# First weight conversions of a fused attention, soft-MoE and MLP kernel moved from GpSimd to VectorE and ScalarE

## Chip, cores and metric

The kernel runs on one core of a Trainium2 chip. The metric is the device time of one execution in microseconds. TensorE does the matmuls, VectorE, ScalarE and GpSimd the elementwise work (in rows of the profile: PE, DVE, ACT and POOL; PEld is TensorE's weight load), and SyncE (SP) issues all the DMAs. Each engine works through its own instructions in order, and waits on semaphores for the others.

## What is computed

The reference chains three stages in float32, cut here to what matters:

```python
k_p, v_p = k.mean over 8 keys, v.mean over 8 keys
attn = softmax(q @ k_p.T / 8) @ v_p
x = attn as (4608 tokens, 512)

logits = x @ phi                       # 32 slots, 4 for each of 8 experts
d = softmax over tokens(logits)
slot_input = d.T @ x
slot_out[e] = relu(slot_input[e] @ w1[e]) @ w2[e]
c = softmax over slots(logits)
x = c @ slot_out

r = relu(x @ w_in)                     # 512 x 2048
out = (s * r * r + b) @ w_out          # 2048 x 512
```

In the last stage x = c @ slot_out has only 32 inner terms. So the kernel does not form x there: it multiplies slot_out into w_in first, S = slot_out @ w_in, and then h = c @ S.

## The kernel before

The attention and the routing come first and are not touched. Then comes the loop over the experts' weights, then the join, then the main loop.

**Experts.** EORD lists 32 weight tiles of 1 MB, and the loop of line 930 takes one in each step (step 0 to step 31). A w1 tile gives products into l1, a w2 tile gives one group of four matmuls into so_ps (line 947). Steps 22 to 31 are w2 tiles. The function hidden turns l1 into the experts' hidden values in three pieces; its last piece is the relu of line 923, and for the second half of the experts it stands at step 23. At the end of every step, step_convs moves each running generator by one piece and starts the next one from the queue todo. That queue holds the generators of combine_t: they take two or fewer tiles of combine weights each, cast them to float32r (cs, line 892), take the remainder on VectorE (line 893), and two steps later transpose both on TensorE (ct, line 898) and copy them to cT (line 904). A transpose is issued between two groups of expert products, so the groups behind it wait when its cs is late.

**Conversions.** The weights w_in and w_out lie in HBM as pairs of 32-bit words. The generator narrow makes float32 numbers of them. VectorE builds the high part in five operations (lines 818 to 828) in th and xp, ScalarE scales the low part into fr (line 830), GpSimd multiplies fr by xp (line 831) and adds it to th (line 832). conv_wi does this for a block of 128 columns of w_in, conv_wo for 128 rows of w_out; conv_wo also splits the result into whi (ScalarE, line 872) and wlo (GpSimd, line 874) and adds it to the column sums wsum (GpSimd, line 876 or 878). The main loop's first group needs two blocks of each (GROUPS[0] is 2). They are put at the front of todo at fixed steps: the two of w_in at steps 23 and 24 (WIPOS), the two of w_out at steps 26 and 27 (WOPOS), these only up to th.

**Join.** After the experts TensorE does two filler matmuls, ScalarE copies so_ps, TensorE sums it up (sot_ps), and then the string OPS orders what follows: `o` moves a w_out generator on by one piece, `a` and `b` are the two matmul steps of s_a and s_b that make a column block S, `h` is st_h (h = cT.T @ S, then relu and square into r), `g` is st_g, which splits r into gh (float32r) and the remainder gl. For step 0 of the main loop all this is done in halves of 384 tokens, the first half's relu and square on ScalarE and the second's on VectorE, and gh and gl of both halves on VectorE.

**Main loop.** Its 96 steps go over five groups of 2, 3, 3, 4 and 4 column blocks, six token blocks of 768 in each. In a step st_o does 18 matmuls of 512 columns (six token tiles, each gh with whi, gl with whi and gh with wlo, line 1073), and st_h and st_r prepare the step after the next. The later conversions are spread over the loop.

SyncE's queue holds the loads in the order of the list loads; a load waits until its buffer is free. Names that readers meet below: ring and raw are buffers of 1 MB (ring tiles that the experts are done with also hold th, xp and fr of the first four conversions), x a further set of such buffers.

The functions that the diff touches:

Of the kernel before, what the change touches and what calls it, by code (L numbers as in the profile page):

```python
# [13 lines left out]
ACTF = mybir.ActivationFunctionType  # L14
ALU = mybir.AluOpType
# [2 lines left out]

OPS = "o0 a0 o0 a1 b0 b1 h0 g0 o1 h1 o1 g1"
WIPOS, WOPOS = 22, 25  # L20
TAIL = "F0 6 C4 X0 D2 6 X1 E2 6 m 6 6 F2 D3 m D4 6 E4 6 m F4 X2 7 W3 7 W2 7 7 7 M2 6 7 7 M3 6 7 M4 7"
BUSY = (2, 0)
CUT = 1
# [33 lines left out]
def kernel(  # L57
# [14 lines left out]
    nc = tc.nc  # L72
# [9 lines left out]
    GROUPS = (2, 3, 3, 4, 4)  # L82
# [10 lines left out]
    raw = [cpool.tile([128, 2048], F32, name=f"raw{i}") for i in range(NRAW)]  # L93
# [12 lines left out]
    where = {}  # L106
# [656 lines left out]
    siz = None  # L763
    for op in TAIL.split():
        if op[0] in "FECD":
# [42 lines left out]
        scr_n[z] += 1  # L808
        return kept[k_][:, o_:o_ + 512].rearrange("p (a x) -> p a x", a=shp[1])

    def narrow(raw, dst):


        v = raw.rearrange("p a (x t) -> p a x t", t=2)
        lo, hi = v[:, :, :, 0], v[:, :, :, 1]
        shp = list(lo.shape)
        th, xp, fr = (scratch_of(z, shp) for z in ("th", "xp", "fr"))
        nc.vector.tensor_scalar(out=xp.bitcast(U32), in0=hi, scalar1=0x7FFFFFFF, scalar2=None, op0=ALU.bitwise_and)
        nc.vector.tensor_scalar(out=xp, in0=xp, scalar1=2.0 ** -15, scalar2=W_MAX, op0=ALU.max, op1=ALU.min)
        nc.vector.tensor_scalar(  # L820
            out=xp.bitcast(U32), in0=xp.bitcast(U32), scalar1=0x07FFFFFF, scalar2=3,
            op0=ALU.bitwise_and, op1=ALU.logical_shift_left,
        )
        nc.vector.scalar_tensor_tensor(
            out=th.bitcast(U32), in0=hi, scalar=0xC0000000, in1=xp.bitcast(U32),
            op0=ALU.bitwise_and, op1=ALU.bitwise_or,
        )
        nc.vector.tensor_scalar(out=xp.bitcast(U32), in0=th.bitcast(U32), scalar1=0xFF800000, scalar2=None, op0=ALU.bitwise_and)
        yield
        nc.scalar.activation(out=fr, in_=lo, func=ACTF.Copy, scale=2.0 ** -52)  # L830
        nc.gpsimd.tensor_tensor(out=fr, in0=fr, in1=xp, op=ALU.mult)  # L831
        nc.gpsimd.tensor_tensor(out=th if dst is None else dst, in0=th, in1=fr, op=ALU.add)  # L832
        yield th

    def conv_wi(f):

        gen = narrow(where["wi", f // 2][2][:, :, 256 * (f % 2):256 * (f % 2) + 256], None)
        next(gen)
        yield
        t = next(gen)  # L840
        if f % 2 == 1:
            done(("wi", f // 2))
        yield
        t_wi[f] = t
# [15 lines left out]

    def conv_wo(f):

        gen = narrow(where["wo", f // 2][2][:, f % 2:f % 2 + 1, :], None)
        next(gen)
        yield
        t = next(gen)[:, 0, :]
        if f % 2 == 1:
            done(("wo", f // 2))
        yield
        g, i = GOF[f]  # L870
        wh, wl = w_hi[g % 2][:, i, :], w_lo[g % 2][:, i, :]
        nc.scalar.copy(out=wh, in_=t)
        yield
        nc.gpsimd.tensor_tensor(out=wl, in0=t, in1=wh.bitcast(F32), op=ALU.subtract)
        if f == 0:
            nc.gpsimd.tensor_copy(out=wsum, in_=t)
        else:
            nc.gpsimd.tensor_tensor(out=wsum, in0=wsum, in1=t, op=ALU.add)

    convs, todo = [], deque()  # L880
# [28 lines left out]
    wo_ = [conv_wo(f) for f in range(GROUPS[0])]  # L909
# [20 lines left out]
    for n_, key in enumerate(EORD):  # L930
        w_, e, hf = key
        g, ge = divmod(e, EG)
        w = where[key][2]
        if w_ == "w1":
            for n in range(2):
                for c in range(2):
                    kc = 2 * hf + c
                    cg = (kc + 2 * n) % 4
                    nc.tensor.matmul(  # L939
                        out=l1[g][n][32 * cg:32 * cg + 32, :],  # L940
                        lhsT=siz[:, 128 * e + 32 * kc:128 * e + 32 * kc + 32],
                        rhs=w[:, c, 512 * n:512 * n + 512],
                        start=(ge == 0), stop=(ge == EG - 1),
                    )
        else:
            for c in range(4):
                nc.tensor.matmul(  # L947
                    out=so_ps[32 * c:32 * c + 32, :],
                    lhsT=h1z[:, 4 * hf + c, 36 * ge + 16 - 4 * e:36 * ge + 48 - 4 * e],
                    rhs=w[:, c, :],  # L950
                    start=(e == 0 and hf == 0), stop=(e == E - 1 and hf == 1),
                )
        done(key, 3 if n_ > 9 else int(n_ > 2))
        if n_ == BRIEF:
            brctx.close()
            cT_t.append(ctx.enter_context(tc.tile_pool(name="cv1", bufs=1, side="right")).tile([128, NTH], F32R, name="cT1"))
        if h1z is None and kept:
            h1z = kept[0][:, 0:1152].rearrange("p (f r) -> p f r", f=8)
            nc.gpsimd.memset(h1z, 0.0)
        advance(hid)  # L960
        if key == W1[g][-1]:
            hid.append(hidden(g))
            advance(hid)
        if WIPOS < n_ <= WIPOS + GROUPS[0]:
            todo.appendleft(conv_wi(n_ - WIPOS - 1))
        if WOPOS < n_ <= WOPOS + GROUPS[0]:
            todo.appendleft(islice(wo_[n_ - WOPOS - 1], 2))
        if key != EORD[-1]:
            step_convs()
    assert not todo, len(todo)  # L970
# [64 lines left out]
    def st_g(i, r):  # L1035
        if i == 0:
            gh = fp2.tile([128, 2, 384], F32R, tag="gh", name="gh")
        else:
            gh = gh_t.pop(i)
        gl = fp2.tile([128, 2, 384], F32R, tag="gl", name="gl")  # L1040
        for x in (slice(0, 1), slice(1, 2)) if i == 0 else (slice(0, 2),):
            if i == 0:
                nc.vector.tensor_copy(out=gh[:, x], in_=r[:, x])  # L1043
            nc.vector.tensor_tensor(out=gl[:, x], in0=r[:, x], in1=gh[:, x].bitcast(F32), op=ALU.subtract)  # L1044
        g_t[i] = (gh, gl)

# [50 lines left out]
    for op in OPS.split():  # L1097
        n = int(op[1])
        if op == "h1":
            r_[1] = st_h(1)  # L1100
            st_r(1, r_[1])
        elif op[0] == "a":
            s_a(n, scratch(2 * n))
        elif op[0] == "b":
            s_b(n, scratch(2 * n + 1))
        elif op[0] == "h":
            r_[n] = st_h(n)
        elif op[0] == "g":
            st_g(n, r_.pop(n))
        elif op[0] == "w":  # L1110
            busy(ps_o.tile([128, 512], F32, tag="o3", name="o3"), n)
        else:
            next(wo_[n], None)
    rctx.close()
    part_p = ctx.enter_context(tc.tile_pool(name="part", bufs=1))
    scr_pool.append(ctx.enter_context(tc.tile_pool(name="scr", bufs=1)))
# [13 lines left out]
    for i in range(len(steps)):  # L1130
        g, blk, fi = steps[i]
# [17 lines left out]
        if t_wi:  # L1149
            f = min(t_wi)  # L1150
# [47 lines left out]
```

## Time and profile before

| | us |
|---|---|
| median of 3 runs | 719.75 |
| lowest and highest | 719.13, 723.48 |
| profiled execution, its own time | 724.16 |
| span in that profile, first to last instruction | 722.0 |
| TensorE busy | 665.4 (92%) |
| VectorE busy | 499.0 (69%) |
| ScalarE busy | 411.4 (57%) |
| GpSimd busy | 297.3 (41%) |

The expert loop ends and the main loop begins between 250 and 280 us of the span. The times of the runs are of whole executions; the span is that of the one that was profiled, and what lies around it is 724.16 less 722.0. In the rows a bracket behind an instruction gives the idle time of its engine just before it and what ended it. PEclk is the granted clock of TensorE as a share of 2.4 GHz, so 0.50 is 1.2 GHz. A float32 matmul leaves two records, so a group of four expert products is counted as x8.

### The profile page before, as it was taken

How to read it: one execution, taken by the hardware profiler on the slowest of the kernel's cores; microseconds unless marked ns; L12 is line 12 of the kernel's file. 1: busy time of each engine (PE TensorE's matmuls, PEld its weight loads, DVE VectorE, ACT ScalarE, POOL GpSimd, SP SyncE). 2: the span in 40 equal slices, each digit the busy share in tenths (PEclk: the TensorE clock that was granted, in tenths of full speed). 3: DMA queues.
4: the chain of work that ended last, by engine and by line, in shares of the span. 5: the costliest groups of instructions: out<-in, count | busy, mean ns of one | idle time of the engine just before them, and what ended most of it. 6: DMA issues, size and time to landing. Idle time of an engine off the chain costs nothing.

```text
span 722.0 us, 11198 instructions
## 1 busy us (share of the span) xinstructions
PE 665.4 (92%) x4294; PEld 522.2 (72%) x4294; DVE 499.0 (69%) x805; ACT 411.4 (57%) x714; POOL 297.3 (41%) x221
## 2 busy tenths in 40 slices
PE   4677889899899978999999999999999999999997
PEld 3566767677763337778888888878788888888885
DVE  6768788667766297788776797888665765456443
ACT  3454666566433345877566666666665666555552
POOL 3646656532210054356132543345331433899100
PEclk9786999899878997999999999999999999999999
DMA  8997446545296980111011110121100000122322
GB/s 302 376 327 223 177 155 198 196 155 203 94 381 241 391 293 33 59 32 58 28 59 59 59 58 1 53 66 59 59 1 0 1 1 1 63 98 90 99 89 88
DMA packets 41317, 88.87 MB, mean 123 GB/s; under 512 B 6960, under 2 KB 15152, under 8 KB 41264
## 3 DMA queue, kind: packets, MB, share of 16 engines
q1 hardware_dynamic: 41264, 88.16, 35.3%
q8 instruction: 34, 0.56, 0.3%
q14 instruction: 19, 0.16, 0.1%
HBM read 78.71 MB, written 9.44 MB: 122 GB/s over the span
## 4 chain that ended last, share of the span: by engine, by line
PE 73%; DVE 16%; ACT 4%; DMA 2%; POOL 2%; issue 2%; SPq 1%; DVEq 0%; POOLq 0%; ACTq 0%
PE o L1073 52%; PE h L1016 4%; PE sc L383 3%; DVE S L393 2%; DVE mx L390 2%; DVE sm L401 2%; PE l L939 2%; DMA ring<-in_v_dram 1%; PE w L434 1%; ACT S L397 1%; PE w L601 1%; PE so_ps L947 1%; DMA brief<-in_moe_w_dram 1%; PE w L578 1%; PE ct L898 1%
## 5 line engine op out<-in xcount | busy, mean ns | idle before, releaser
L1073 PE MATMUL o<-whi,gh 128*128 128x512 f32 x576 | 229.4, 399 | 2.5 <-DVE gh L1043 2.5
L1073 PE MATMUL o<-whi,gl 128*128 128x512 f32 x576 | 225.5, 392 | 0.8 <-DVE gl L1044 0.7
L1073 PE MATMUL o<-wlo,gh 128*128 128x512 f32 x576 | 225.6, 392 | 0.0
L1025 ACT ACTIVATE r<-h 128x768 f32<-128x768 f32 x95 | 77.2, 813 | 152.7 <-PE h L1016 149.0
L1044 DVE TENSOR_TENSOR gl<-r,gh 128x768 fp32r<-128x768 f32 (+1 forms) x97 | 114.5, 1181 | 63.2 <-ACT gh L1033 62.8
L1086 DVE SCALAR_TENSOR_TENSOR part<-o,sb_t,part 128x512 f32<-128x512 f32 x144 | 99.6, 743 | 50.4 <-PE o L1073 47.8
L1073 PEld LDWEIGHTS o<-whi,gh 128*128 128x128 f32 x576 | 108.8, 189 | 24.1 <-issue 5.8
L1073 PEld LDWEIGHTS o<-wlo,gh 128*128 128x128 f32 x576 | 108.7, 189 | 24.1
L1073 PEld LDWEIGHTS o<-whi,gl 128*128 128x128 f32 x576 | 108.8, 189 | 21.6 <-DVE gl L1044 2.8
L831 POOL TENSOR_TENSOR fr<-fr,xp 128x512 f32<-128x512 f32 x28 | 41.1, 1467 | 183.3 <-ACT fr L830 161.2
L1026 ACT ACTIVATE r<-r 128x768 f32<-128x768 f32 x95 | 80.5, 847 | 3.0
L1033 ACT CAST gh<-r 128x768 fp32r<-128x768 f32 x95 | 79.5, 836 | 2.4
L421 POOL TENSOR_TENSOR P<-S,rs 128x576 f32<-128x576 f32 x32 | 37.3, 1166 | 82.9 <-DVE rs L404 42.0
L1167 POOL TENSOR_TENSOR part<-part,wsum 128x512 f32<-128x512 f32 x36 | 53.3, 1521 | 10.5 <-ACT wsum L1161 10.5
L1016 PE MATMUL h<-cT,S 128*128 128x384 f32 x192 | 49.7, 342 | 0.5 <-DVE S L859 0.5
L383 PE MATMUL sc<-kb,qT 128*128 128x144 f32 x256 | 44.3, 325 | 0.0
L832 POOL TENSOR_TENSOR th<-th,fr 128x512 f32<-128x512 f32 x28 | 43.0, 1537 | 2.2
L1016 PEld LDWEIGHTS h<-cT,S 128*128 128x128 f32 x192 | 36.7, 192 | 8.2 <-DVE S L859 0.7
L390 DVE TENSOR_REDUCE mx<-sc 128x8 f32<-128x576 f32 x36 | 26.4, 734 | 20.6 <-PE sc L383 17.3
L383 PEld LDWEIGHTS sc<-kb,qT 128*128 128x128 f32 x256 | 40.0, 223 | 0.4 <-ACT qT L355 0.2
L401 DVE TENSOR_REDUCE sm<-S 128x8 f32<-128x576 f32 x36 | 27.0, 750 | 18.3 <-ACT S L397 18.2
L397 ACT ACTIVATE S<-S 128x576 f32<-128x576 f32 x36 | 24.5, 682 | 25.2 <-DVE S L393 25.2
(211 smaller groups left out, 910.2 us busy)
## 6 DMA issues: line engine op xcount, KB each, us to landing
ring<-in_moe_w_dram SPq DMA_DIRECT2D x14, 1024.0 KB, 7.6
x<-in_moe_w_dram SPq DMA_DIRECT2D x13, 1024.0 KB, 9.8
raw<-in_moe_w_in_dram SPq DMA_DIRECT2D x8, 1024.0 KB, 5.6
raw<-in_moe_w_out_dram SPq DMA_DIRECT2D x8, 1024.0 KB, 4.9
out_dram<-part SPq DMA_DIRECT2D x32, 256.0 KB, 2.5
ring<-in_q_dram SPq DMA_DIRECT2D x7, 1024.0 KB, 9.6
ring<-in_v_dram SPq DMA_DIRECT2D x9, 768.0 KB, 9.8
ring<-in_k_dram SPq DMA_DIRECT2D x7, 768.0 KB, 7.0
```

The costliest lines, as they stand in the source:

```text
L383: nc.tensor.matmul(out=sc[:, i // 2, 2 * KP * (i % 2):2 * KP * (i % 2) + 2 * KP], lhsT=qT[:, i, :], rhs=kb[:, H * bb + 4 * (j % 2) + i, :] ...
L401: nc.vector.tensor_reduce(out=sm, in_=S, axis=AX.X, op=ALU.add)
L831: nc.gpsimd.tensor_tensor(out=fr, in0=fr, in1=xp, op=ALU.mult)
L832: nc.gpsimd.tensor_tensor(out=th if dst is None else dst, in0=th, in1=fr, op=ALU.add)
L1016: nc.tensor.matmul(out=h[x][:, 0:384] if i == 0 else h[:, x, 0:384], lhsT=Sw_t[f], rhs=cT(c, 384), start=True, stop=True)
L1025: nc.scalar.activation(out=r, in_=h[:, :, 0:384], func=ACTF.Relu)
L1026: nc.scalar.activation(out=r, in_=r, func=ACTF.Square)
L1033: nc.scalar.copy(out=gh_t[i], in_=r)
L1044: nc.vector.tensor_tensor(out=gl[:, x], in0=r[:, x], in1=gh[:, x].bitcast(F32), op=ALU.subtract)
L1073: nc.tensor.matmul(out=o_t[tt], lhsT=l[:, x, 128 * c:128 * c + 128], rhs=r, start=(fi == 0 and n == 0), stop=(fi == GROUPS[g] - 1 and n == 2),
L1086: nc.vector.scalar_tensor_tensor(out=p, in0=o_t[tt], scalar=sb_t[:, 0:1], in1=p, op0=ALU.mult, op1=ALU.add)
L1167: nc.gpsimd.tensor_tensor(out=p, in0=p, in1=wsum, op=ALU.add)
```

## The change

The four first conversions do their product and sum on VectorE (narrow gets the engine as an argument; for all later ones it stays GpSimd), and for them ScalarE's scaling is issued in the same piece as VectorE's five operations. They start at steps 23, 24, 25 and 26 (CONV) and no longer at 23, 24, 26 and 27. In st_g the first half's gh of step 0 is a copy on ScalarE, issued ahead of VectorE's cast of the second half. For the first group conv_wo gives up once more between wlo and the column sum, and a loop behind OPS runs those generators out, so both sums are issued after both wlo.

```diff
 WIPOS, WOPOS = 22, 25
+
+CONV = 23
...
-    def narrow(raw, dst):
+    def narrow(raw, dst, eng):
...
-        yield
-        nc.scalar.activation(out=fr, in_=lo, func=ACTF.Copy, scale=2.0 ** -52)
-        nc.gpsimd.tensor_tensor(out=fr, in0=fr, in1=xp, op=ALU.mult)
-        nc.gpsimd.tensor_tensor(out=th if dst is None else dst, in0=th, in1=fr, op=ALU.add)
+        if eng is nc.vector:
+            nc.scalar.activation(out=fr, in_=lo, func=ACTF.Copy, scale=2.0 ** -52)
+        yield
+        if eng is nc.gpsimd:
+            nc.scalar.activation(out=fr, in_=lo, func=ACTF.Copy, scale=2.0 ** -52)
+        eng.tensor_tensor(out=fr, in0=fr, in1=xp, op=ALU.mult)
+        eng.tensor_tensor(out=th if dst is None else dst, in0=th, in1=fr, op=ALU.add)
         yield th
...
-        gen = narrow(where["wi", f // 2][2][:, :, 256 * (f % 2):256 * (f % 2) + 256], None)
+        gen = narrow(where["wi", f // 2][2][:, :, 256 * (f % 2):256 * (f % 2) + 256], None, nc.vector if f < GROUPS[0] else nc.gpsimd)
...
         nc.gpsimd.tensor_tensor(out=wl, in0=t, in1=wh.bitcast(F32), op=ALU.subtract)
+        if g == 0:
+            yield
         if f == 0:
...
-        if WIPOS < n_ <= WIPOS + GROUPS[0]:
-            todo.appendleft(conv_wi(n_ - WIPOS - 1))
-        if WOPOS < n_ <= WOPOS + GROUPS[0]:
-            todo.appendleft(islice(wo_[n_ - WOPOS - 1], 2))
+        if CONV <= n_ < CONV + GROUPS[0]:
+            todo.appendleft(conv_wi(n_ - CONV))
+        elif CONV <= n_ < CONV + 2 * GROUPS[0]:
+            todo.appendleft(islice(wo_[n_ - CONV - GROUPS[0]], 2))
...
+        if i == 0:
+            nc.scalar.copy(out=gh[:, 0], in_=r[:, 0])
+            nc.vector.tensor_copy(out=gh[:, 1], in_=r[:, 1])
         for x in (slice(0, 1), slice(1, 2)) if i == 0 else (slice(0, 2),):
-            if i == 0:
-                nc.vector.tensor_copy(out=gh[:, x], in_=r[:, x])
             nc.vector.tensor_tensor(out=gl[:, x], in0=r[:, x], in1=gh[:, x].bitcast(F32), op=ALU.subtract)
...
+    for gen in wo_:
+        next(gen, None)
     rctx.close()
```

VectorE's instructions around the last cs tile (the one with two blocks of 32, cs_3021), before. The ring names are the buffers of th (ring5) and of xp and fr (ring7), raw0 holds w_in and raw2 w_out:

```order
L818 TENSOR_SCALAR ring7_86<-raw0_65 128x512
L819 TENSOR_SCALAR ring7_86<-ring7_86 128x512
L820 TENSOR_SCALAR ring7_86<-ring7_86 128x512
L824 SCALAR_TENSOR_TENSOR ring5_84<-raw0_65,ring7_86 128x512
L828 TENSOR_SCALAR ring7_86<-ring5_84 128x512
L893 TENSOR_TENSOR cs_3021<-L3_75,cs_3021 128x2x32
L818 TENSOR_SCALAR ring7_86<-raw2_67 128x512
```

The same on VectorE after the change, where that tile is called cs_3046:

```order
L820 TENSOR_SCALAR ring7_86<-raw2_67 128x512
L821 TENSOR_SCALAR ring7_86<-ring7_86 128x512
L822 TENSOR_SCALAR ring7_86<-ring7_86 128x512
L826 SCALAR_TENSOR_TENSOR ring5_84<-raw2_67,ring7_86 128x512
L830 TENSOR_SCALAR ring7_86<-ring5_84 128x512
L836 TENSOR_TENSOR ring7_86<-ring7_86 128x512
L837 TENSOR_TENSOR ring5_84<-ring5_84,ring7_86 128x512
L900 TENSOR_TENSOR cs_3046<-L3_75,cs_3046 128x2x32
L864 TENSOR_TENSOR S0_3094<-o1_3135,S0_3094 64x128
```

Each conversion has become seven operations, and the cs tile has gone from behind the second conversion to behind the fourth, just ahead of the column S.

TensorE's instructions at the end of the expert loop, before (so_ps are the experts' products, ct the transposes of cs, and the last row is the filler behind step 31):

```order
L898 MATMUL ct_3001<-ident_60,cs_2980 128x128 x2
L947 MATMUL so_ps_2683<-ring4_83,ring0_79 32x512 x4
L947 MATMUL so_ps_2683<-ring2_81,ring0_79 32x512 x4
L947 MATMUL so_ps_2683<-ring3_82,ring0_79 32x512 x4
L898 MATMUL ct_3037<-ident_60,cs_3021 128x128
L947 MATMUL so_ps_2683<-raw1_66,ring0_79 32x512 x4
L947 MATMUL so_ps_2683<-x_2137,ring0_79 32x512 x4
L947 MATMUL so_ps_2683<-x_2138,ring0_79 32x512 x4
L947 MATMUL so_ps_2683<-x_2139,ring0_79 32x512 x4
L975 MATMUL l1_2684<-cT0_2668 128x512 x2
```

The same on TensorE after the change:

```order
L905 MATMUL ct_3002<-ident_60,cs_2980 128x128 x2
L954 MATMUL so_ps_2683<-ring4_83,ring0_79 32x512 x4
L954 MATMUL so_ps_2683<-ring2_81,ring0_79 32x512 x4
L954 MATMUL so_ps_2683<-ring3_82,ring0_79 32x512 x4
L954 MATMUL so_ps_2683<-raw1_66,ring0_79 32x512 x4
L954 MATMUL so_ps_2683<-x_2137,ring0_79 32x512 x4
L905 MATMUL ct_3058<-ident_60,cs_3046 128x128
L954 MATMUL so_ps_2683<-x_2138,ring0_79 32x512 x4
L954 MATMUL so_ps_2683<-x_2139,ring0_79 32x512 x4
L982 MATMUL l1_2684<-cT0_2668 128x512 x2
```

The last transpose stands two groups later: five groups go ahead of it since the one before, where there were three, and two groups stand behind it instead of four.

## Rows read from the trace of the kernel before

**Rows 1.** Page, costliest groups: busy and mean | idle before, and its releaser.

```profile
L1073 PE MATMUL o<-whi,gh 128*128 128x512 f32 x576 | 229.4, 399 | 2.5 <-DVE gh L1043 2.5
...
L1073 PE MATMUL o<-wlo,gh 128*128 128x512 f32 x576 | 225.6, 392 | 0.0
...
L831 POOL TENSOR_TENSOR fr<-fr,xp 128x512 f32<-128x512 f32 x28 | 41.1, 1467 | 183.3 <-ACT fr L830 161.2
```

**Rows 2.** TensorE's timeline, 254 to 274 us: start, length, engine, line, operation.

```profile
254.49 2.78 PE L947 MATMUL so_ps<-ring,ring 128*32 128x512 f32 x24
259.66 0.33 PE L898 MATMUL ct<-ident,cs 128*128 128x128 f32 x1 [2.38 <-DVE cs L893]
259.92 1.06 PE L947 MATMUL so_ps<-raw,ring 128*32 128x512 f32 x8
...
263.49 0.73 PE L975 MATMUL l<-cT 128*128 128x512 f32 x2
264.26 1.08 PE L982 MATMUL sot_ps<-sel,si_all 128*128 128x32 f32 x8
...
272.97 0.77 PE L1073 MATMUL o<-whi,gh 128*128 128x512 f32 x1 [2.47 <-DVE gh L1043]
```

**Rows 3.** VectorE's timeline, 252 to 278 us, the same columns.

```profile
252.59 0.42 DVE L818 TENSOR_SCALAR ring<-raw 128x512 uint32<-128x512 uint32 x1
...
255.03 0.42 DVE L818 TENSOR_SCALAR ring<-raw 128x512 uint32<-128x512 uint32 x1
...
255.95 1.39 DVE L820 TENSOR_SCALAR ring<-ring 128x512 uint32<-128x512 uint32 x1
...
259.38 0.22 DVE L893 TENSOR_TENSOR cs<-L,cs 128x64 fp32r<-128x64 f32 x1
...
265.75 1.37 DVE L820 TENSOR_SCALAR ring<-ring 128x512 uint32<-128x512 uint32 x1
...
267.88 0.43 DVE L828 TENSOR_SCALAR ring<-ring 128x512 uint32<-128x512 uint32 x1
...
270.49 0.99 DVE L1023 TENSOR_TENSOR r<-r 128x384 f32<-128x384 f32 x1
271.41 1.42 DVE L1043 CAST gh<-r 128x384 fp32r<-128x384 f32 x1
...
277.41 0.42 DVE L818 TENSOR_SCALAR xp<-raw 128x512 uint32<-128x512 uint32 x1
```

**Rows 4.** Instructions on the tile raw: shortest, median, longest ns, starts, shapes.

```profile
L250 DVE TENSOR_TENSOR raw<-raw x5: 557/560/986, 33.9 to 138.0; 128x384 f32<-128x384 f32 x5
```

**Rows 5.** TensorE after an earlier gap; windows: length, busy of five engines, PEclk, DMA.

```profile
68.87 0.39 PE L545 MATMUL w<-ident,md 128*32 128x128 f32 x1 [4.57 <-DVE md L538]
...
67.00:68.00 1.00, 0.00 (x0) 0.00 (x0) 0.90 (x2) 0.00 (x0) 0.86 (x1) 0.77 0.98 302
74.00:75.00 1.00, 1.00 (x7) 0.65 (x6) 0.97 (x2) 0.95 (x4) 0.92 (x2) 0.81 0.00 0
268.00:270.00 2.00, 1.54 (x8) 1.34 (x7) 0.93 (x4) 0.91 (x3) 1.47 (x2) 0.73 0.39 82
278.00:280.00 2.00, 2.00 (x8) 1.68 (x8) 1.83 (x4) 0.57 (x1) 0.00 (x0) 0.71 0.00 0
```

**Rows 6.** TensorE's timeline, two pairs of the main loop's first step.

```profile
276.06 1.05 PE L1073 MATMUL o<-whi,gh 128*128 128x512 f32 x2
276.92 1.05 PE L1073 MATMUL o<-whi,gl 128*128 128x512 f32 x2
```

**Rows 7.** ScalarE's timeline in the join.

```profile
266.87 0.62 ACT L872 CAST whi<-ring 128x512 fp32r<-128x512 f32 x1 [1.23 <-POOL ring L832]
...
270.10 0.52 ACT L1022 ACTIVATE r<-r 128x384 f32<-128x384 f32 x1
```

**Rows 8.** SyncE's timeline, 250 to 320 us.

```profile
259.07 2.34 SPq L136 DMA_DIRECT2D raw<-in_moe_w_in_dram  x2
267.91 24.86 SPq L136 DMA_DIRECT2D raw<-in_moe_w_out_dram  x2
```

More of the change, by code (lines that the diff above doesn't have):

```diff
@@ L861, in conv_wo @@
     def conv_wo(f):
-        gen = narrow(where["wo", f // 2][2][:, f % 2:f % 2 + 1, :], None)
+        gen = narrow(where["wo", f // 2][2][:, f % 2:f % 2 + 1, :], None, nc.vector if f < GROUPS[0] else nc.gpsimd)
         next(gen)
```

## Prediction

> **What bounds the kernel now.** I read the page's costliest groups first, then the timelines of TensorE, VectorE and ScalarE around the one place where the diff acts, then the granted clock there. The first row of [rows 1] says how little TensorE waits in its main loop: 2.5 us before the 576 products of whi with gh, all of it for one thing, gh of line 1043; the products with wlo wait 0.0. So the loop (272.97 to the end) is bound by TensorE, and nothing in it is for sale but its start. The join between the experts and the loop is where time lies [rows 2]: the experts' products run back to back to about 257.3, TensorE then stands 2.38 us for a cs tile of VectorE (the last transpose of the combine weights), does four more groups of expert products, and starts the three matmuls of the tail (sot_ps, the column S, h) at 263.49. The first loop matmul comes at 272.97, 9.5 us after the experts' end.
>
> What runs beside it [rows 3]: VectorE starts the first conversion at 252.59 and needs 2.44 us for its five operations when it is alone (252.59 to 255.03). From then on GpSimd's products run too, and six of the later operations take 1.4 us or more instead of 0.4 to 0.7: the first and the last of the six are shown, at 255.95 and 265.75. At 0.95 too much in each, the excess is 5.7 us. The last conversion ends at 268.3 only because of that. The last cs stands in the middle, at 259.38, after two conversions.
>
> **VectorE's new queue.** Twenty of its operations stay, and each conversion gets a product and a sum, eight more. The trace has no such operation at 128x512 on VectorE. The nearest is the 128x384 sum with both operands in SBUF at 0.557 us alone [rows 4]; in proportion to the columns 512 would be 0.74, and with a fixed part in it less. I take 0.7, and 0.73 from start to start. Bounds: 0.42 (the 128x512 rows with one tensor, as at 252.59) and 1.2 (between the contended 384-wide rows at 270.49 and 271.41).
>
> A conversion is then 2.44 + 2 x 0.73 = 3.9 us, four are 15.6, and from 252.59 they end at 268.2. That is where the last one ends today: 8 x 0.72 = 5.8 us come, 5.7 us of contention go. What is new is the place of the last cs. The piece that makes it is started at step 27 of the expert loop instead of 25, behind all 28 conversion operations, as the order shows. It is 0.22 us long and lands at 268.4 instead of 259.6. With the bounds of 0.42 and 1.2 it lands at 266 or 272.
>
> ScalarE's four scalings are issued earlier than they are today. The third and fourth wait for buffers that VectorE frees with the first and second conversion, by about 256.5 and 260.4; their products come two conversions, 7.8 us, behind those. None is late.
>
> **TensorE's wait.** Four groups of expert products took 263.49 - 259.92 = 3.57 us, 0.89 each. TensorE passes the groups of steps 25 to 29 from 254.49 on, is through at about 259.0, and then stands before the transpose that reads cs. It goes on at 268.5. Behind that transpose in its queue are the last two groups, without which there is no so_ps; for so_ps wait ScalarE's copy, sot_ps, and all of the tail. At full clock they end at 268.5 + 0.25 + 1.79 = 270.5, against 263.5 today: +7.0 us.
>
> **The clock.** TensorE idles 9.5 us there. In this trace the granted clock fell in the course of gaps half as long: in the 4.57 us before 68.87 the row 67 to 68 has a mean of 0.77, and the clock came back in the row 74 to 75, some 6 us after work resumed [rows 5]. So TensorE restarts at 1.2 GHz: the two groups take 3.6 us instead of 1.8 and the transpose 0.1 more (+1.9), and sot_ps, today 1.08 us, some 0.7 more. After about 6 us, near 274.5, the clock would be back; then the first h pair, which runs at half clock today (268 to 270 has a mean of 0.73), gains 0.3. In the tail TensorE works little, as today, so the clock should fall once more before the loop starts, and the first matmuls run at 0.43 us from start to start [rows 6] until some 6 us later, as today. I price that part at nothing, with bounds of -2.4 (twelve matmuls at twice the clock) and +1.
>
> **What the tail gains.** ScalarE stands 1.23 us before its cast of the first whi because th comes late from GpSimd, and the copies of sps queue behind that cast [rows 7]. With th ready the cast fits under s_a's matmuls: 1.0 us (bounds 0.6 and 1.2). Then gh. Today VectorE does the product r at 0.99 and the cast of the first half at 1.42, both beside GpSimd, and gh is ready at 272.83. Now ScalarE, which ends its square at 270.62, does that half in 0.5 us as its other 384-wide operations: ready at 271.1, 1.7 earlier. The second loop matmul needs gl, behind r at 0.56 instead of 0.99 and a cast of some 0.4 instead of 1.42: 1.45 earlier by these two, and a bit more for gl itself without a neighbour. I take 1.6 for both. A dear case, with GpSimd's wlo beside all three, is 0.3. Together -2.6 us.
>
> The Trainium skill's page "SBUF — State Buffer" (section "Who interferes with whom") says that VectorE and GpSimd share one pair of ports and that a two-input VectorE operation can be shut out for the whole of a GpSimd instruction that reads SBUF. The six rows above agree. For this change it also speaks against it: the second wlo now starts next to the first gl, and by the rule that gl could stand for the length of that wlo, which would take the gain of gl to about nothing.
>
> **Edits that cost nothing.** The column sums stand behind both wlo on GpSimd; the first wlo is not waited for today, and the second is used by step 1 of the loop, six microseconds after its start. The added loop that runs the generators out only emits those sums. On SP's queue the third w_in load now takes the slot that the last w_out conversion frees, and the next w_out load stands behind it: it goes out near 266.5, not at 267.91 [rows 8], and the w_in load, one of the two from 259.07 on, slips to there. The loop's first conversion reads at 277.41 a tile that was loaded earlier [rows 3], and these two come two and more conversions later: covered by over 10 us. If not, a conversion would be late, not a matmul.
>
> **The sum.** +7.0 + 1.9 + 0.7 - 0.3 - 2.6 = +6.7 us. On the profiled execution (724.16, of which the span is 722.0) that is 730.9. The median of the three runs shown is 719.75, 4.4 lower; the same stretch is in every run, so I put the sum on it: 726.4.
>
> **Rivals.**
> B, the low clock lasts. From the restart TensorE stays at 1.2 GHz through s_a, s_b and h and comes back 2.3 us later in the loop than today. Then sot_ps costs its whole 1.1, s_a and s_b 0.3, the h pair gains nothing, five loop matmuls lose 0.2 each: +7.0 + 1.9 + 1.1 + 0.3 + 1.0 - 2.6 = +8.7, 728.5. For it: the work after the two groups is broken, and the return in [rows 5] came under unbroken work. Against it: sot_ps and the two groups fill some 6 us without a hole. It decides if the clock is still low at 276.
> C, the clock comes back and stays. The tail is shorter now, and the clock holds at 2.4 GHz into the loop: A less 2.4, +4.3, 724.0. For it: the dense restart lies nearer to the loop. Against it: today's tail starts at 263.49 and has lost the clock by 270.
> D, TensorE is not held at all, and only the tail counts: -2.6, 717.2. That needs the conversions done before about 260, at 0.27 us for each of 28 operations, or a cs that does not queue behind them. Against it stand the durations and the order in one queue. It is the case of not slower, and would be decided at the start of the transpose: at 260 or at 268.
>
> The skill's page "GPSIMD Engine Reference" (section 4.1, Engine selection) sends an elementwise product to VectorE, as GpSimd takes about twice as long. The product of line 831 has a mean of 1467 ns on GpSimd [rows 1], twice the 0.7 taken here, so the durations agree. Read as advice for this change it predicts D; it leaves out what else waits in VectorE's queue.
>
> **How the numbers follow.** A 0.45 (its own range 725 to 728), B 0.30, C 0.20, D 0.05. The line between no change and slower is 1%, 7.2 us, about what a measurement of this kernel can tell from no change: 726.9, just above A. Of A a third lies above it, of B nine in ten: 0.40 for slower. Faster by over 1% would need 712.6, below even D: 0.02. The rest, 0.58, is within 1%. With the bounds of the product's price (-2.3 and +4), of the tail (2.3 less) and of the clock in the loop, eight in ten lie between 722.0 and 730.0.
>
> **What would show it.** Right: on VectorE 28 conversion operations in a row, none over 0.8 us, ending near 268.2, cs behind them; TensorE idle some 9 us before the last transpose of ct, released by cs; a granted clock of 0.5 when so_ps goes on; the experts' end between 271.5 and 273; then under 7.5 us to the first loop matmul, with gh from ScalarE; the loop itself unchanged. Wrong: the transpose starts near 260 (D), products over 1 us each (cs at 270 or later), or a loop that waits for a conversion because a load slipped.

## The result, and the profile after

The changed kernel takes 728.43 us (median of 4 runs, 726.58 to 732.90); the kernel before took 720.12 beside it (4 runs, 719.13 to 723.48). The ratio is 1.012, with a 95% interval of 1.0085 to 1.0155: slower, by 1.2%. In the experiments below the kernel before ran 31, 31 and 13 times more, with medians of 721.95, 722.35 and 721.96; against those some 722 us, taken at other times and on three chips, the change costs 6.4 us, 0.9%.

The profiled execution of the changed kernel took 726.58 us, 724.6 of it span. Its costliest groups, which answer to [rows 1]:

```profile
L1081 PE MATMUL o<-whi,gh 128*128 128x512 f32 x576 | 229.4, 399 | 0.7 <-ACT gh L1049 0.7
...
L1081 PE MATMUL o<-wlo,gh 128*128 128x512 f32 x576 | 225.2, 391 | 0.0
...
L836 POOL TENSOR_TENSOR fr<-fr,xp 128x512 f32<-128x512 f32 x28 | 41.1, 1468 | 181.5 <-ACT fr L835 159.5 <-DVE xp L830 10.8 <-DVE S L864 6.6
```

The main loop is what it was: busy times within 0.4 us, and TensorE waits even less before its first product (0.7 us, now for ScalarE's gh, where it was 2.5). What was lost lies ahead of it. VectorE's timeline, which answers to [rows 3]:

```profile
249.20 0.42 DVE L820 TENSOR_SCALAR ring<-raw 128x512 uint32<-128x512 uint32 x1
...
251.83 0.69 DVE L836 TENSOR_TENSOR ring<-ring 128x512 f32<-128x512 f32 x1
...
264.47 0.69 DVE L837 TENSOR_TENSOR ring<-ring,ring 128x512 f32<-128x512 f32 x1
265.08 0.22 DVE L900 TENSOR_TENSOR cs<-L,cs 128x64 fp32r<-128x64 f32 x1
...
275.91 0.36 DVE L1050 CAST gh<-r 128x384 fp32r<-128x384 f32 x1
276.18 2.10 DVE L1052 TENSOR_TENSOR gl<-r,gh 128x384 fp32r<-128x384 f32 x2
```

28 conversion operations stand in a row from 249.20 on, the new products and sums at 0.69 each, and the last cs behind all of them. TensorE's timeline, which answers to [rows 2], shows who waits for it:

```profile
254.56 1.04 PE L954 MATMUL so_ps<-x,ring 128*32 128x512 f32 x8
265.36 0.48 PE L905 MATMUL ct<-ident,cs 128*128 128x128 f32 x1 [9.75 <-DVE cs L900]
265.76 3.64 PE L954 MATMUL so_ps<-x,ring 128*32 128x512 f32 x16
269.33 1.14 PE L982 MATMUL l<-cT 128*128 128x512 f32 x2
270.31 0.97 PE L989 MATMUL sot_ps<-sel,si_all 128*128 128x32 f32 x8
...
273.68 1.65 PE L1023 MATMUL h<-cT,S 128*128 128x384 f32 x4 [0.46 <-DVE S L864]
276.04 0.80 PE L1081 MATMUL o<-whi,gh 128*128 128x512 f32 x1 [0.72 <-ACT gh L1049]
276.79 0.80 PE L1081 MATMUL o<-whi,gl 128*128 128x512 f32 x1
```

TensorE stands 9.75 us where it stood 2.38, and the two groups behind the wait take 269.33 - 265.76 = 3.57 us. The windows of the same stretch (columns as in [rows 5]; the number behind the five engines is the granted clock) say why:

```profile
255.00:257.00 2.00, 0.60 (x8) 0.00 (x0) 1.83 (x4) 0.00 (x0) 0.00 (x0) 1.00 0.91 288
...
259.00:261.00 2.00, 0.00 (x0) 0.00 (x0) 1.83 (x4) 0.00 (x0) 0.00 (x0) 0.75 0.41 155
...
265.00:267.00 2.00, 1.65 (x9) 0.58 (x13) 0.30 (x2) 0.27 (x1) 0.00 (x0) 0.50 0.96 332
267.00:269.00 2.00, 2.00 (x12) 0.20 (x4) 0.00 (x0) 0.00 (x0) 0.00 (x0) 0.50 1.06 427
269.00:271.00 2.00, 2.00 (x13) 1.40 (x10) 0.00 (x0) 0.59 (x1) 0.00 (x0) 0.69 0.58 236
271.00:273.00 2.00, 1.42 (x23) 1.04 (x22) 0.00 (x0) 1.22 (x4) 0.76 (x1) 1.00 0.00 0
...
275.00:277.00 2.00, 1.28 (x4) 0.50 (x3) 1.93 (x5) 1.97 (x4) 0.41 (x1) 0.50 0.00 0
277.00:279.00 2.00, 2.00 (x5) 1.62 (x6) 1.30 (x2) 1.90 (x3) 1.92 (x3) 0.50 0.00 0
279.00:281.00 2.00, 2.00 (x7) 1.55 (x6) 2.00 (x2) 0.00 (x0) 1.11 (x1) 0.63 0.00 0
281.00:283.00 2.00, 2.00 (x11) 1.70 (x10) 1.86 (x5) 1.29 (x2) 0.00 (x0) 1.00 0.00 0
```

TensorE falls from 2.4 to 1.2 GHz in the gap, comes back in the row 269 to 271, falls again among the short waits of the tail, and starts the main loop at 1.2 GHz.

To compare executions I count from VectorE's first conversion, which I call t0: what lies ahead of it is the same code in all kernels, yet t0 itself stands between 246.93 us (e2) and 257.62 us (e6) in the profiles of this study. Each row is one execution. All in us from t0 (the experts' end is the start of the two filler matmuls behind them; the end is the end of the span):

| kernel | last cs starts | its transpose starts (wait) | experts' end | h | first loop product | second | end |
|---|---|---|---|---|---|---|---|
| before | 6.79 | 7.07 (2.38) | 10.90 | 16.29 | 20.38 | 21.17 | 469.41 |
| after | 15.88 | 16.16 (9.75) | 20.13 | 24.48 | 26.84 | 27.59 | 475.40 |
| e1_cs_middle | 7.94 | 8.22 (3.52) | 12.05 | 17.43 | 19.80 | 20.55 | 468.11 |
| e2_place_only | 15.47 | 15.75 (9.34) | 19.73 | 24.12 | 26.72 | 28.22 | 476.67 |
| e3_gh_only | 6.80 | 7.07 (2.38) | 12.60 | 16.93 | 19.05 | 21.20 | 468.42 |
| e4_filler | 15.89 | 16.16 (1.37) | 18.27 | 22.52 | 24.64 | 25.24 | 472.52 |
| e5_cs_early | 3.97 | 4.24 (0.41) | 10.45 | 14.95 | 17.07 | 17.81 | 465.38 |
| e6_wo1_late | 3.97 | 4.25 (0.41) | 10.41 | 14.65 | 16.77 | 17.75 | 467.28 |
| e7_cs_early_filler | 3.97 | 4.24 (0.41) | 10.01 | 15.03 | 17.09 | 17.69 | 464.80 |
| e8_one_edit | 3.97 | 4.24 (0.41) | 9.90 | 17.57 | 19.93 | 20.68 | 469.40 |
| e9_gh_vector | 15.88 | 16.15 (9.75) | 20.13 | 24.38 | 26.61 | 27.11 | 474.76 |
| e10_sums_between | 15.88 | 16.16 (9.75) | 20.13 | 24.42 | 26.79 | 27.54 | 475.46 |
| e11_before_filler | 6.80 | 7.07 (2.38) | 12.48 | 16.82 | 20.41 | 21.20 | 467.95 |

From t0 to the end the change costs 475.40 - 469.41 = 6.0 us. The spans differ by only 2.6, because t0 came 3.4 earlier in the one profile than in the other.

### The profile page after: what moved, and what is told of

Same layout as the page of the kernel before. It is cut to its first block, busy times and chain, and to the rows that moved or that the text cites. A ratio compares the mean times of both kernels' runs of the same rounds, so it can differ in the third digit from the quotient of the medians.

```text
span 724.6 us, 11195 instructions
## 1 busy us (share of the span) xinstructions
PE 661.0 (91%) x4294; PEld 517.3 (71%) x4294; DVE 498.4 (69%) x812; ACT 411.8 (57%) x715; POOL 286.1 (39%) x213
## 4 chain that ended last, share of the span: by engine, by line
PE 73%; DVE 16%; ACT 4%; POOL 2%; issue 2%; DMA 1%; SPq 1%; DVEq 0%; ACTq 0%; POOLq 0%
PE o L1081 52%; PE h L1023 4%; PE sc L385 2%; PE l L946 2%; DVE S L395 2%; DVE mx L392 2%; DVE sm L403 2%; PE so_ps L954 1%; DMA ring<-in_v_dram 1%; ACT S L399 1%; PE w L436 1%; PE w L603 1%; PE w L580 1%; PE ct L905 1%; PE w L459 1%
## 5 line engine op out<-in xcount | busy, mean ns | idle before, releaser
L385 PE MATMUL sc<-kb,qT 128*128 128x144 f32 x256 | 42.2, 313 | 0.0
L385 PEld LDWEIGHTS sc<-kb,qT 128*128 128x128 f32 x256 | 38.1, 214 | 0.3 <-ACT qT L357 0.2
```

The source lines that it names most:

```text
L385: nc.tensor.matmul(out=sc[:, i // 2, 2 * KP * (i % 2):2 * KP * (i % 2) + 2 * KP], lhsT=qT[:, i, :], rhs=kb[:, H * bb + 4 * (j % 2) + i, :] ...
```

## The experiments

The times, each with its ratio to the kernel before on the same chip:

| kernel | median us (runs) | ratio, 95% |
|---|---|---|
| e1_cs_middle | 721.21 (10) | 1.0001, 0.9974 to 1.0028 |
| e2_place_only | 727.78 (10) | 1.0078, 1.0042 to 1.0114 |
| e3_gh_only | 723.83 (10) | 1.0027, 1.0001 to 1.0054 |
| e4_filler | 724.81 (10) | 1.0046, 1.0015 to 1.0077 |
| e5_cs_early | 720.01 (12) | 0.9961, 0.9933 to 0.9989 |
| e6_wo1_late | 721.67 (12) | 0.9987, 0.9959 to 1.0015 |
| e7_cs_early_filler | 718.19 (8) | 0.9932, 0.9903 to 0.9961 |
| e8_one_edit | 722.84 (12) | 0.9998, 0.9966 to 1.0029 |
| e9_gh_vector | 728.55 (1) | single run, no interval |
| e10_sums_between | 730.61 (1) | single run, no interval |
| e11_before_filler | 719.48 (10) | 0.9965, 0.9931 to 0.9999 |

**The place of cs, from both sides.** e1 keeps the changed kernel's engines and starts w_out's conversions one step later, at 26 and 27 as before, so that cs stands behind two conversions again. e2 takes the kernel before, with its products on GpSimd, and starts them one step earlier, at 25 and 26, so that cs stands behind four.

```diff
e1, of after
-        elif CONV <= n_ < CONV + 2 * GROUPS[0]:
-            todo.appendleft(islice(wo_[n_ - CONV - GROUPS[0]], 2))
+        elif CONV + 3 <= n_ < CONV + 3 + GROUPS[0]:
+            todo.appendleft(islice(wo_[n_ - CONV - 3], 2))
e2, of before
-        if WOPOS < n_ <= WOPOS + GROUPS[0]:
-            todo.appendleft(islice(wo_[n_ - WOPOS - 1], 2))
+        if WOPOS <= n_ < WOPOS + GROUPS[0]:
+            todo.appendleft(islice(wo_[n_ - WOPOS], 2))
```

> The changed kernel with the w_out conversions at steps 26 and 27 again, so that the last cs stands between the second and the third conversion; the conversions stay on VectorE. Theory 1 (the queue: TensorE is held by a cs that stands behind all conversions): cs lands about 8 us after the first conversion starts, TensorE stands 3 to 3.5 us before the last transpose, the clock is not lost there, and from the start of the first conversion to the first matmul of the main loop it takes 18.7 us (before 20.4, changed kernel 26.8); time about 718, 8 to 10 us under the changed kernel. Theory 2 (the engine: VectorE is the dearer place for the products and sums, wherever cs stands): the stretch stays above 24 us and the time within 3 us of the changed kernel.

> The kernel before with one edit: the two w_out conversions start at steps 25 and 26, so the last cs stands behind all four conversions; products and sums stay on GpSimd, gh on VectorE. Theory 1 (the queue): cs lands about 15.6 us after the first conversion starts although GpSimd does the products, TensorE stands over 9 us, and the stretch to the first loop matmul is 27 to 28.5 us; time 7 to 10 us over the kernel before. Theory 2 (the engine): no product is on VectorE, so the stretch stays near the 20.4 us of before, at most 22, and the time within 2 us.

e2 has the loss without the new engine, and e1 the new engine without the loss. TensorE's wait in e2, and then in e1:

```profile
262.68 0.48 PE L898 MATMUL ct<-ident,cs 128*128 128x128 f32 x1 [9.34 <-DVE cs L893]
```

```profile
257.91 0.33 PE L905 MATMUL ct<-ident,cs 128*128 128x128 f32 x1 [3.52 <-DVE cs L900]
```

From t0 to the end e2 takes 7.3 us more than before, and its time is 0.8% up (under the 7 to 10 us expected); e1 takes 1.3 less and its time is the same, not the 718 expected. So it is the place in the queue that costs, not the length of the operations. The four kernels add up: the place costs 7.3 us with GpSimd's products (476.67 - 469.41) and 7.3 with VectorE's (475.40 - 468.11), and the rest of the change gains 1.3 us in either place. In e1 the first loop product came at 19.80 where 18.7 was expected, and VectorE, GpSimd and TensorE show the reason (in that order):

```profile
264.38 0.69 DVE L836 TENSOR_TENSOR ring<-ring 128x512 f32<-128x512 f32 x1
265.11 1.64 DVE L837 TENSOR_TENSOR ring<-ring,ring 128x512 f32<-128x512 f32 x1
266.78 0.50 DVE L864 TENSOR_TENSOR S<-o,S 64x128 fp32r<-64x128 f32 x2
```

```profile
264.55 1.64 POOL L879 TENSOR_TENSOR wlo<-ring,whi 128x512 fp32r<-128x512 f32 x1 [43.34 <-DMA raw<-in_moe_w_in_dram]
```

```profile
267.12 1.65 PE L1023 MATMUL h<-cT,S 128*128 128x384 f32 x4 [1.59 <-DVE S L864]
```

The last sum takes 1.64 us instead of 0.69, and the column S waits behind it. With the first whi early, GpSimd's first wlo runs beside that sum.

**The clock in the gap.** e4 is the changed kernel with 36 filler matmuls ahead of the last transpose; they write a tile that nobody reads.

```diff
+        if n_ == 29:
+            for _ in range(36):
+                nc.tensor.matmul(out=l1[0][0], lhsT=cT(0, 128), rhs=cT(0, 512), start=True, stop=True)
```

> The changed kernel with 36 filler matmuls (8.2 us at full clock) on TensorE ahead of the last transpose, into a tile nobody reads: the hold of TensorE stays, its idleness goes. Theory of the prediction (the idle gap costs the clock, +1.9 us for the two groups of expert products): granted clock 1.0 when so_ps goes on, the two groups in 1.8 us instead of 3.6, stretch to the first loop matmul 24.5 to 25.3 us instead of 26.8. Rival (the two groups are slow for another reason, such as late weights): they stay at 3.6 us and the stretch at 26.8.

```profile
255.11 8.45 PE L977 MATMUL l<-cT 128*128 128x512 f32 x36
264.94 0.33 PE L905 MATMUL ct<-ident,cs 128*128 128x128 f32 x1 [1.37 <-DVE cs L900]
265.20 1.93 PE L954 MATMUL so_ps<-x,ring 128*32 128x512 f32 x16
```

```profile
265.00:267.00 2.00, 2.00 (x17) 0.50 (x17) 0.00 (x0) 0.27 (x1) 0.00 (x0) 1.00 0.98 369
```

The transpose comes at the same 16.16 from t0, the clock is at 1.00 behind it, and the same two groups take 267.05 - 265.20 = 1.85 us (267.05 is where the next instruction starts) and not 3.57. The experts' end is 1.86 earlier, the end 2.9. So the clock's part of the loss in the gap is 1.9 us, the wait's the rest; a clock that was never lost also helped the tail (h takes 0.97 instead of 1.65).

**The gh edit by itself.** e3 is before with only st_g's edit; e9 is after without it.

```diff
e3, of before (e9 is the reverse, of after)
+        if i == 0:
+            nc.scalar.copy(out=gh[:, 0], in_=r[:, 0])
+            nc.vector.tensor_copy(out=gh[:, 1], in_=r[:, 1])
         for x in (slice(0, 1), slice(1, 2)) if i == 0 else (slice(0, 2),):
-            if i == 0:
-                nc.vector.tensor_copy(out=gh[:, x], in_=r[:, x])
```

> The kernel before with the edit of st_g alone: the first half's gh of step 0 on ScalarE. Theory of the prediction: the first loop matmul comes 1.3 to 1.7 us earlier (stretch 18.8 to 19.1 instead of 20.4), time about 718.5. Rival (whi and the remainder gl bind the loop's start as well, VectorE's product beside GpSimd stays slow): the first matmul is earlier but the second waits for gl, and the loop gains under 0.7 us.

> The changed kernel with st_g as before: gh of both halves on VectorE. If the edit of gh is worth what the prediction put on it, the way from the experts' end to the first loop matmul goes from 6.7 us back to 7.2 to 8.2 us (VectorE is free of GpSimd's products now, so less than the 1.7 us counted comes back), and TensorE waits for gh of VectorE. If the tail's gain came from whi and a free VectorE alone, it stays at 6.7 to 6.9.

TensorE in e3 and then in e11 (the kernel before with fillers, further down), then VectorE in e9:

```profile
273.23 0.50 PE L1074 MATMUL o<-whi,gh 128*128 128x512 f32 x1 [1.16 <-ACT gh L1042]
275.38 0.79 PE L1074 MATMUL o<-whi,gl 128*128 128x512 f32 x1 [1.64 <-DVE gl L1045]
```

```profile
274.66 0.47 PE L1073 MATMUL o<-whi,gh 128*128 128x512 f32 x1 [1.23 <-DVE gh L1043]
```

```profile
277.57 0.56 DVE L1030 TENSOR_TENSOR r<-r 128x384 f32<-128x384 f32 x1
278.05 0.35 DVE L1050 CAST gh<-r 128x384 fp32r<-128x384 f32 x1
278.43 0.56 DVE L1051 TENSOR_TENSOR gl<-r,gh 128x384 fp32r<-128x384 f32 x1
```

VectorE does r in 0.56 and the cast in 0.35 in e9, where [rows 3] has 0.99 and 1.42. e9 starts the loop 0.2 earlier than the changed kernel and ends 0.6 earlier, but its h ran at full clock (0.98 us instead of 1.65), so its 6.48 us from the experts' end to the first product, under both ranges expected, do not decide. Four runs whose h ran at full clock can be compared, in us from the start of h to the first and to the second loop product (from the table above):

| | GpSimd's last conversion beside it | no conversion on GpSimd |
|---|---|---|
| gh on VectorE | 3.59, 4.38 (e11) | 2.23, 2.73 (e9) |
| first gh on ScalarE | 2.12, 4.27 (e3) | 2.12, 2.72 (e4) |

For the first product either edit is enough, and the second adds only 0.1 us. The second product needs gl, and there the copy on ScalarE is worth 0.1 us or less, and a VectorE without GpSimd's conversion beside it some 1.6. So what the loop's start gained came from GpSimd's silence, not from ScalarE's copy. e3's time does not follow its trace: the trace ends 1.0 us earlier from t0, the time is 0 to 0.5% longer, where 718.5 us was expected. Which part of the program holds that is open.

**The order of the sums.** e10 is after without the extra yield, so each column sum stands behind its own wlo.

```diff
-        if g == 0:
-            yield
```

> The changed kernel with the column sums issued behind each wlo again. By the prediction the order of the sums costs nothing: first loop matmul at 26.8 us after the first conversion, the loop's second step starts at the same distance, within 0.3 us. Rival: the sum runs beside r, gh and gl on VectorE and costs them 0.5 us or more.

First loop product at 26.79 instead of 26.84, end at 475.46 instead of 475.40: worth nothing here.

**cs ahead of three conversions.** If the place costs, a better place should gain. e8 changes only the steps, so that cs stands behind the first conversion alone. e5 also takes the product and sum of the last conversion out of the expert loop and reorders OPS; e6 takes all of that conversion out and leaves it to be started in the tail.

```diff
e8, of after
-        if CONV <= n_ < CONV + GROUPS[0]:
-            todo.appendleft(conv_wi(n_ - CONV))
-        elif CONV <= n_ < CONV + 2 * GROUPS[0]:
-            todo.appendleft(islice(wo_[n_ - CONV - GROUPS[0]], 2))
+        if n_ in (CONV, CONV + 2):
+            todo.appendleft(conv_wi((n_ - CONV) // 2))
+        elif CONV + 3 <= n_ < CONV + 5:
+            todo.appendleft(islice(wo_[n_ - CONV - 3], 2))
e5, of after: the last two lines are instead
+        elif n_ == CONV + 3:
+            todo.appendleft(islice(wo_[0], 2))
+        elif n_ == CONV + 4:
+            todo.appendleft(islice(wo_[1], 1))
+OPS = "a0 a1 b0 b1 o0 o0 h0 g0 o1 h1 o1 g1 o1"
e6: as e5 without the wo_[1] branch
+OPS = "a0 a1 b0 b1 o0 o0 h0 g0 o1 o1 h1 o1 g1 o1"
```

> The changed kernel with the last cs behind the first conversion and nothing else moved. Theory 1: TensorE's hold goes to under 1 us, but S waits for VectorE's fourth conversion (15.8 us), so the first loop matmul comes at 18.5 to 20 us after the first conversion starts, about 1 us better than before and 7 better than the changed kernel. Theory 2 (the engine): above 24.

> The changed kernel with three moves: the last cs stands behind the first conversion; the product and sum of the last w_out conversion come behind both gl; the first whi is cast behind S instead of ahead of sps. Theory 1 (the queue): TensorE stands under 1 us before the last transpose, the experts end 9.0 to 9.6 us after the first conversion starts, VectorE is free for S at 14.3, and the first loop matmul comes at 17.0 to 17.5 us (before 20.4, changed kernel 26.8); from the first conversion to the end of the span 3 us less than before; time 717 to 719. Theory 2 (the tail from the experts' end is fixed at 7 us whatever VectorE does): the first matmul comes at 16.2.

> As the run before, but all of the last w_out conversion stands behind both gl, so VectorE has nothing queued ahead of S. Theory 1: S no longer waits for VectorE, the first loop matmul comes at 15.0 to 15.5 us after the first conversion starts; the price appears in step 1 of the loop, which waits 1 to 2 us for the second whi and wlo; to the end of the span 3.5 to 4.5 us less than before. Theory 2 (the clock or the weights hold the tail): the first matmul stays at 17.

TensorE in e5, and then in e8:

```profile
257.76 0.33 PE L905 MATMUL ct<-ident,cs 128*128 128x128 f32 x1 [0.41 <-DVE cs L900]
...
262.97 1.06 PE L954 MATMUL so_ps<-x,ring 128*32 128x512 f32 x8 [1.31 <-DMA x<-in_moe_w_dram]
...
270.59 0.50 PE L1083 MATMUL o<-whi,gh 128*128 128x512 f32 x1 [1.16 <-ACT gh L1051]
```

```profile
266.67 1.65 PE L1023 MATMUL h<-cT,S 128*128 128x384 f32 x4 [3.84 <-DVE S L864]
```

The wait for cs is gone in all three (0.41 us). What is late next is the weights of the last expert group, 0.76 to 1.31 us, so the experts end only 0.4 to 1.0 us sooner than before. In e8 the four conversions still end in front of the column S in VectorE's queue, h waits 3.84 us for it, and the end is where it was before. With the last piece behind S (e5) the loop starts 3.3 us sooner than before and the end is 4.0 sooner; its time is 0.1 to 0.7% lower, at 720.01 us a little above the 717 to 719 expected. In e6 the loop starts 0.3 sooner still (at 16.77, where 15.0 to 15.5 was expected), but the late conversion is paid for in the loop: from the h of step 2 to that of step 3 it takes 5.08 us and from there to that of step 4 6.22, where 4.45 is the usual; the end is 1.9 later than e5's. What e5's order would give with the products still on GpSimd was not tried, so how much of its 4.0 us is the new engine's is open.

**Holding the clock through the tail.** e11 is before with two and six filler matmuls in OPS; e7 is e5 with six and two. Again the fillers write a tile that nobody reads.

```diff
e11, of before
-OPS = "o0 a0 o0 a1 b0 b1 h0 g0 o1 h1 o1 g1"
+OPS = "o0 a0 o0 a1 b0 b1 w2 h0 g0 o1 h1 w6 o1 g1"
e7, of e5
+OPS = "a0 a1 b0 b1 w6 o0 o0 h0 g0 o1 h1 w2 o1 g1 o1"
both
-            busy(ps_o.tile([128, 512], F32, tag="o3", name="o3"), n)
+            busy(ps_o.tile([128, 512], F32, tag="o0", name="o0"), n)
```

> The kernel before with eight filler matmuls in the holes of its tail, two ahead of h and six between h and the first loop matmul, and nothing else. If the low clock at the loop's start is a price of TensorE's idle tail by itself, the clock holds to the loop and from the first conversion to the end of the span it is 2 to 2.7 us shorter than before (469.4 to about 467); time 719 to 720 beside a before of 722. If the fillers only helped together with the early cs, the span is unchanged.

> The kernel with cs early and the last product late, plus eight filler matmuls in the tail's holes (six ahead of h, two behind it), into a tile that is overwritten. If the clock is lost because TensorE works little in the tail, it now stays at 1.0 to the loop: the first twelve loop matmuls go at 0.23 us instead of 0.43, and the span behind the first conversion is 2 to 2.7 us shorter than without fillers. If it is lost anyway, the fillers change nothing or delay h by up to 0.5 us.

Windows of e11, of e7 and of e5, in that order:

```profile
262.00:264.00 2.00, 2.00 (x12) 0.40 (x8) 1.97 (x2) 0.67 (x2) 1.92 (x2) 0.50 0.92 260
...
274.00:276.00 2.00, 1.02 (x3) 0.67 (x4) 1.97 (x3) 1.79 (x3) 2.00 (x3) 1.00 0.01 2
276.00:278.00 2.00, 1.58 (x7) 0.90 (x5) 1.97 (x2) 0.00 (x0) 1.90 (x2) 1.00 0.00 0
```

```profile
268.00:270.00 2.00, 1.91 (x8) 1.37 (x8) 1.97 (x4) 1.94 (x3) 0.00 (x0) 1.00 0.60 244
270.00:272.00 2.00, 2.00 (x11) 1.72 (x10) 1.89 (x3) 1.24 (x3) 1.14 (x1) 1.00 0.00 0
```

```profile
272.00:274.00 2.00, 2.00 (x6) 1.57 (x5) 1.97 (x4) 1.57 (x3) 0.20 (x1) 0.50 0.03 8
```

With the fillers the loop starts at 2.4 GHz in both. In e11 the first product stands where it stood (20.41), and the end is 1.5 us sooner (2 to 2.7 were expected); the next h, that of step 2, comes 4.51 us behind the first product and not 5.65. In e7 it comes 3.21 us behind it, in e5 4.86; of those 1.65 us only 0.6 remain at the end (again 2 to 2.7 were expected), since gl is now late for a faster TensorE once more:

```profile
278.39 0.50 PE L1083 MATMUL o<-whi,gl 128*128 128x512 f32 x1 [0.83 <-DVE gl L1054]
```

e7 is the fastest of all: 718.19 us, 0.4 to 1.0% below the kernel before, and 4.6 us less from t0 to the end. It beats both kernels.

## Why the prediction was right in its cause and close in its sum

**VectorE's queue: right.** Forecast were 15.8 us from t0 until cs lands and operations of 0.7; cs landed at 15.88 + 0.22 = 16.1, and the operations took 0.69. e1 and e2 show that the place in the queue alone decides the wait.

**TensorE's wait: right.** A wait of 9.5 us was forecast and 9.75 measured, released by cs; rival D, no wait, is out. The Trainium skill's page "GPSIMD Engine Reference" (section 4.1, Engine selection), read as advice, holds for the length of the product (0.69 us on VectorE, 1.47 on GpSimd) and leaves out the queue. The whole change but the place of cs gains 1.3 us from t0 to the end, and the place costs 7.3.

**The clock on the two groups: right.** 3.57 us, forecast 3.6; e4 isolates it. With the wait's 7.0 that made +8.9 at the experts' end, measured 20.13 - 10.90 = +9.2.

**sot_ps +0.7 and the h pair -0.3: both failed.** They rested on a clock that comes back some 6 us after the restart. It came back in the row 269 to 271, some 4.9 us after it (0.69 in that row): sot_ps took 0.97 (1.08 before). Then it fell once more in the tail, so h took 1.65 at half clock, as before (1.62). The two are -0.1 and 0 in place of +0.7 and -0.3. The -0.3 was also too small for its own case: at full clock h takes 0.97 (e4), 0.65 less.

**The tail: right in size, wrong in cause for the most part.** From the experts' end to h 4.35 us against 5.39: -1.0, as forecast for whi and sps. From h to the first loop product 2.36 against 4.09: -1.7, forecast 1.6. The prediction put this down to GpSimd having no conversions left and to ScalarE's copy of gh. But e2, where GpSimd still has the products and VectorE all of gh, has 4.39 and 2.60, so 2.5 of these 2.8 us come without either move. In e2, as in the changed kernel, the tail starts about 9 us later from t0, when the conversions are over on whichever engine has them: whi does not wait, and VectorE works undisturbed up to the first gh, as e2's cast shows (1.42 in [rows 3]):

```profile
273.16 0.35 DVE L1043 CAST gh<-r 128x384 fp32r<-128x384 f32 x1
```

So the tail gave back part of the wait because it came late. What the engine and the copy add there is 0.3 us at the first product and 1.0 at the second (7.46 us from the experts' end, in e2 8.49).

**The loop's start: priced at nothing, came out at -0.5.** From the first loop product to the end 448.56 us against 449.03. The clock was back some 4.4 us after the start of the loop instead of 6.2 (from the 0.63 in the row 279 to 281 and the 0.71 in [rows 5]), inside the bounds given. Rival B wanted a loop that loses more, rival C a clock that stays at 2.4 GHz; neither came. e11 shows what C would have been worth: 1.5 us, not 2.4.

**The sum.** +9.2 - 2.8 - 0.5 = +6.0 us from t0, forecast +6.7: the main terms held. Against the forecast sot_ps is 0.8 and the loop's start 0.5 lower, the experts' end and the h pair 0.3 higher each. The medians first compared differ by 8.3 us, but against the kernel before in its later runs it is 6.4. That 728.43 is also the 728.5 of rival B is chance: the clock was back by sot_ps and came back sooner in the loop than before, and from t0 the loss is 6.0 us, not B's 8.7. The 728.43 measured lies within the range, and over the line of 1% that the forecast stood 0.5 us below; with an interval of 0.85 to 1.55% that line is not clearly passed. The likeliest side, no change, was the wrong one by a little: the sum was put on a median of three runs, and the spread of the runs is wider than the distance of the sum from the line.

**Edits that cost nothing: right.** The order of the sums is worth 0.1 us (e10). The next w_out load went out at 263.71, 14.5 us behind t0 where 13.9 was forecast, and no product of the loop waited for a conversion.

**The rule on the shared ports** (the Trainium skill's page "SBUF — State Buffer", section "Who interferes with whom") was to take the gain of gl. Its effect is there: the pair of gl takes 2.10 us beside the wlo that starts at 276.59, against 0.55 for one alone. But the first gl runs ahead of that wlo, the second product follows the first by 0.75, and the neighbour hit is the second half, which TensorE does not yet need. GpSimd in the changed kernel:

```profile
276.59 1.29 POOL L879 TENSOR_TENSOR wlo<-ring,whi 128x512 fp32r<-128x512 f32 x1 [3.09 <-ACT whi L877]
```

In e1 the same effect hits a sum that TensorE does need. So the rule is right on the length, and the order of issue says who pays. The prediction also set six rows beside it as agreeing; five of the six are operations with one input (such as those at 255.95 and 265.75) and only one has two (257.37, 1.63 us), so for the two-input case they are one row and not six.

## What to carry to other kernels

When work moves to an engine, list what else stands in that engine's queue and who waits for it: here a cs operation of 0.22 us behind 15.9 us of conversions cost 7.3 us, and all that the rest of the change gave back was 1.3. Then move that small operation first and ask what is late next; here it was a load, the column S, and the clock. A gap as long as the 9.75 us here is to be priced twice, once as time and once as the half clock behind it, and fillers in a gap that can't be closed gave back the second part. A gain seen behind such a wait need not belong to the change: here most of the tail's gain was there as well when only the order was changed.

## What was not expected of the hardware

The 2.38 us gap before the last transpose left the clock at 1.00 in the profile of before, where its four groups took 3.57 us:

```profile
262.00:264.00 2.00, 2.00 (x18) 0.56 (x10) 1.93 (x4) 1.09 (x2) 0.51 (x1) 1.00 1.04 378
```

In e3 and e11, whose code is the same up to there, the clock fell in the same gap (0.50 in the row 262 to 264 of e11 above), the first group of four products behind it took 1.94 us instead of 1.06, and the experts ended 1.6 to 1.7 us later. In e1 a longer gap, 3.52 us, left the clock at 1.00, so the length of the gap alone does not decide; what does was not tried. The loss did not reach the loop: e11's first product stands at 20.41 from t0 and before's at 20.38, and TensorE waits there for VectorE's gh in both (1.23 and 2.47 us).

t0 differs by up to 10.7 us between executions of code that is the same up to there. A change of a few microseconds in one stage is therefore seen in the interval from the stage's start in one trace, while the time of ten runs still has an interval of about 0.3%, 2 us, to either side.
